# Placing attention, gates and slot copies on a fixed line of MoE half-steps, with the row-tiled work of a half in one step

## The chip, the cores and the metric

The kernel runs on one core of one Trainium2 chip. The metric is the device time of one execution in microseconds (us). A time quoted is the median of three to seven executions. The span that a profile page gives is about 1.7 us shorter than the device time of the same execution. Times inside an execution are counted from the start of its span.

Five engines share the work: PE (TensorE, matmuls), DVE (VectorE), ACT (ScalarE), POOL (GpSimd, which here also issues the loads of the experts' weights) and SP (SyncE, which issues the other transfers).

## The reference, cut to what matters

Eight sequences pass through an attention whose softmaxes are taken of q and of k apart. A gate then picks one expert for each sequence, and the sequence passes through the two matrices of that expert.

```python
def _attn_ref(q, k, v):                      # 8 sequences, 8 heads, 576 rows, 64 columns
    q_s = softmax of q over its 64 columns
    k_s = softmax of k over the 576 rows
    kv = np.einsum('bhsd,bhse->bhde', k_s, v)
    return np.einsum('bhsd,bhde->bhse', q_s, kv)

def _moe_ref(x, w_gate, w1, w2):             # x: 8 x 576 x 512, w1: 8 x 512 x 1024
    pooled = x.mean(axis=1)
    logits = pooled @ w_gate
    e_idx = np.argmax(logits, axis=1)        # one expert for each sequence
    ...
        h = np.maximum(x[mask] @ w1[e], 0.0)
        out[mask] = gate_w[mask, None, None] * (h @ w2[e])
```

The sequences pick the experts 2 3 3 1 3 3 4 6. So sequences 0, 1, 3, 6 and 7 need new weights. Sequences 2, 4 and 5 find theirs in the core's memory.

## The kernel before

A sequence is worked in two halves of four heads each. For a half, q, k and v are loaded; ACT takes exponentials, POOL casts v and scales q; PE forms k^T v (`kv_step`), transposes q (`t_step`) and multiplies both to x (`x_step`). DVE evacuates x and sums it for the gate. To evacuate is to copy a result out of the bank in which matmuls left it; the next matmul that needs this bank waits until then. The row sum, also on DVE, is the sum of q's exponentials over their 64 columns, by which POOL then scales q.

```python
    def t_step(n, g):                        # one partition half g of the half n
        eq = halves[n]["eq"]
        r = slice(64 * g, 64 * g + 64)
        tp = kv_banks(n)[g].bitcast(FP16)[:, 448:448 + S]
        for j in range(J):                   # J = 9
            nc.tensor.transpose(out=tp[:, 64 * j:64 * j + 64], in_=eq[r, j], identity=ident[r, r])
        ...
```

The gate finds the expert. If an earlier sequence has loaded the same expert, the loads are skipped by a condition. Five slots hold weights. Before the MoE block of sequence b, DVE copies the weights of its source slot into slot b % 5, in two parts for w1 and two for w2. The source slot is known only on the chip, so it is read by a register:

```python
    def gate_step(b):
        ...                                  # on DVE: the expert, and the slot that holds it
        nh = 1 if b else 2
        for fh in range(nh):
            for i in range(2):
                for h in range(2):
                    nc.gpsimd.dma_start(out=w1_all[..., slot, ...], in_=w1_src[i, h][...], **kw)
        ...                                  # then load_w2(b): two loads of w2; kw holds the condition

    def fetch(b, w_all, part):               # the slot copy
        ...
        cs = slice(part * half, (part + 1) * half)
        nc.vector.tensor_copy(
            out=w_all[:, b % NS, cs],
            in_=w_all[:, ds(seqs[b]["src"], 1), cs].rearrange("p o c f -> p (o c) f"),
        )
```

The MoE block is a generator of 17 half-steps. Between them, the program runs the attention, gate and copies that are due on a line of ticks, 12 ticks to a sequence. The order written here is the order of each engine's instructions.

```python
    NA = 12
    for b in range(B):
        for i in range(2 if b else 0):
            n, t0 = 2 * b + i, NA * b + 5 * i
            at(t0, kv_step, n)
            for g in range(2):
                at(t0 + 1 + g, t_step, n, g)
                at(t0 + 3 + g, x_step, n, g)
        at(NA * b + 10, gate_step, b)
        ...
            for part in range(2):
                at(NA * (b + 1) + 6 + part, fetch, b, w1_all, part)
                at(NA * (b + 1) + 8 + part, fetch, b, w2_all, part)
    for n in range(4, 2 * B):
        t0 = NA * (n // 2) + 5 * (n % 2)
        ...                                  # exp_q, cast_v, exp_k, load(n + 3), scale_q ahead of t0
    ...
        for b in range(B):
            for m, _ in enumerate(moe(b)):
                goal = NA * (b + 2) + 10     # attention two sequences ahead of MoE
                left = units - m
                tick = min(tick + max(0.7, (goal - tick) / left), NA * (b + 3))
                run_ticks(tick)
```

The copies of sequence b stand at ticks 12b + 18 to 12b + 21, and the gate of the next sequence at 12b + 22.

The softmax here doesn't subtract the row's maximum and nothing guards it: scores larger than these inputs give would overflow.

Of the kernel before, what the change touches and what calls it, by code (L numbers as in the profile page):

```python
# [19 lines left out]
def kernel(  # L20
# [54 lines left out]
    nc.vector.memset(ones_f32, 1.0)  # L75
    ones_row = consts.tile([1, 128], FP16)
# [3 lines left out]
    held = consts.tile([1, 8], FP16)  # L80
# [75 lines left out]
    def kv_step(n):  # L156
        ek, va, kps = halves[n]["ek"], v_aug[n % NVB], kv_banks(n)
        for j in range(J):
            for g in range(2):
                r = slice(64 * g, 64 * g + 64)  # L160
                nc.tensor.matmul(  # L161
                    kps[g][:, 0:129], lhsT=ek[r, j], rhs=va[r, j],
                    start=(j == 0), stop=(j == J - 1),
                )
        for g in range(2):
            icv = kv_pool.tile([128, 1], FP32, name="icv")
            nc.vector.reciprocal(out=icv, in_=kps[g][:, 0:1])
            kv = kv_pool.tile([128, 128], FP16, name="kv")
            nc.vector.scalar_tensor_tensor(
                out=kv, in0=kps[g][:, 1:129], scalar=icv, in1=blkmask, op0=ALU.mult, op1=ALU.mult,  # L170
            )
            halves[n]["kv"][g] = kv

    def t_step(n, g):
        eq = halves[n]["eq"]
        r = slice(64 * g, 64 * g + 64)
        tp = kv_banks(n)[g].bitcast(FP16)[:, 448:448 + S]
        for j in range(J):
            nc.tensor.transpose(out=tp[:, 64 * j:64 * j + 64], in_=eq[r, j], identity=ident[r, r])  # L179
        qt = qt_pool.tile([128, S], FP16, name="qt")  # L180
        if n < 2:
            nc.scalar.copy(qt, tp)
        else:
            nc.vector.tensor_copy(out=qt, in_=tp)  # L184
        halves[n]["qt"][g] = qt

    def x_step(n, g):
        b, i = divmod(n, 2)
        c = 2 * i + g
        if c == 0:  # L190
            xt = xt_pool.tile([128, ND, S], FP16, name="xt")
            pooled = gat_pool.tile([128, ND], FP32, name="pooled")
            seqs[b] = {"xt": xt, "pooled": pooled}
        xt, pooled = seqs[b]["xt"], seqs[b]["pooled"]
        kvs, qts = halves[n]["kv"], halves[n]["qt"]
        px = bank("x")
        nc.tensor.matmul(px[:, 0:SM], lhsT=kvs[g], rhs=qts[g][:, 0:SM], start=True, stop=True)  # L197
        nc.tensor.matmul(px[:, SM:S], lhsT=kvs[g], rhs=qts[g][:, SM:S], start=True, stop=True)  # L198
        nc.vector.tensor_tensor_reduce(  # L199
            out=xt[:, c, :], in0=px[:, 0:S], in1=ones_f32.to_broadcast([128, S]),  # L200
            scale=1.0, scalar=0.0, op0=ALU.mult, op1=ALU.add, accum_out=pooled[:, c:c + 1],
        )

    def gate_step(b):
        pooled = seqs[b]["pooled"]
        pg = bank("x")
# [61 lines left out]
    def hold_loads():  # L268

        nc.sync.dma_start(out=held, in_=w1_all[64:65, 0, ND - 1, 0:8])  # L270
# [97 lines left out]
    NA = 12  # L368
# [5 lines left out]
    for b in range(B):  # L374
        for i in range(2 if b else 0):
            n, t0 = 2 * b + i, NA * b + 5 * i
            at(t0, kv_step, n)
            for g in range(2):
                at(t0 + 1 + g, t_step, n, g)
                at(t0 + 3 + g, x_step, n, g)  # L380
        at(NA * b + 10, gate_step, b)
        late = 0 if b else 5
        at(NA * b + 11 + late, gate_exp, b)
        at(NA * b + 12 + late, gate_split, b)
        at(NA * b + 14 + late, gate_spread, b)
        if b:
            for part in range(2):
                at(NA * (b + 1) + 6 + part, fetch, b, w1_all, part)
                at(NA * (b + 1) + 8 + part, fetch, b, w2_all, part)
    at(15, load_w2, 0)  # L390
    for n in range(4, 2 * B):
        t0 = NA * (n // 2) + 5 * (n % 2)
        x = 3 if n == 4 else 0
        at(t0 - 6 + x, exp_q, n)
        at(t0 - 6 + x, cast_v, n)
        at(t0 - 5 + x, exp_k, n)
        if n + 3 < 2 * B:
            at(t0 - 5 + x, load, n + 3)
        at(t0 - 4 + (x and 2), scale_q, n, nc.gpsimd)
# [16 lines left out]
    with tc.manual_schedule(engines={ET.PE, ET.DVE, ET.Activation, ET.Pool, ET.SP}):  # L416

        exp_q(0)
# [6 lines left out]
        t_step(0, 0)  # L425
        t_step(0, 1)
# [4 lines left out]
        t_step(1, 0)  # L431
        t_step(1, 1)
        x_step(0, 1)
        kv_step(1)
        cast_v(2)
        x_step(1, 0)
        exp_q(2)
        x_step(1, 1)
        exp_k(2)
        run_ticks(11)  # L440
        hold_loads()
        load(4)
        scale_q(2, nc.vector)
        exp_q(3)
        run_ticks(13)
        exp_k(3)
        cast_v(3, True)
        load(5)
        run_ticks(15)
        scale_q(3, nc.vector)  # L450
        tick = NA + 6.0
        run_ticks(tick)
        load(6)
        for b in range(B):
            units = 17
            for m, _ in enumerate(moe(b)):
                goal = NA * (b + 2) + 10
                left = units - m
                tick = min(tick + max(0.7, (goal - tick) / left), NA * (b + 3))
                run_ticks(tick)  # L460
# [30 lines left out]
```

## Time and profile before

| | before |
|---|---|
| median, 3 runs | 232.39 us (231.48 to 233.29) |
| span of the profiled execution | 230.8 us |
| PE busy | 179.8 us, 78% of the span |
| start of MoE blocks 0, 1, 2, 3 | 32.5, 74.6, 95.8, 127.9 us |
| end of PE | 225.8 us |

The prediction shows the views that carry its argument. One more is needed for the comparison: the windows view of the kernel before, cut at the starts of single MoE blocks. Each line is a stretch and its length; then the busy time of PE, of PE's weight loads, of DVE, ACT and POOL, with instruction counts in brackets; then the granted PE clock (the share of TensorE's full clock that the profile shows as let through), the DMA share and GB/s.

```profile
74.55:95.77 21.22, 21.22 (x203) 11.17 (x202) 13.02 (x44) 12.62 (x20) 6.28 (x10) 0.99 0.75 222
127.85:149.70 21.85, 21.85 (x203) 11.32 (x203) 13.04 (x44) 12.62 (x20) 6.28 (x10) 0.96 0.51 147
149.70:171.20 21.50, 21.11 (x204) 11.14 (x203) 14.29 (x46) 12.62 (x20) 7.01 (x10) 1.00 0.41 116
171.20:193.50 22.30, 21.09 (x204) 11.12 (x203) 14.18 (x47) 10.62 (x18) 9.54 (x9) 1.00 0.79 151
193.50:209.92 16.42, 16.42 (x122) 8.33 (x123) 3.60 (x19) 8.79 (x16) 3.94 (x6) 1.00 0.82 140
```

Compare a line's length with PE's busy time. In these blocks (1 and 3 to 6) the two differ by at most 1.2 us, and the clock is nearly full. Here PE is the bound. Block 6, with no attention beside it, is 16.4 us, and the attention of a further sequence adds about 5 us.

### The profile page before, as it was taken

What the parts mean: (1) busy time and instruction counts of PE and PEld (TensorE: products, weight loads), DVE (VectorE), ACT (ScalarE), POOL (GpSimd) and SP (SyncE); (2) the same over time, 40 slices, a digit from 0 to 9 for tenths busy, and PEclk for the clock granted to TensorE, in tenths of its full rate; (3) what the DMA queues carried; (4) which work ended last, traced back from release to release, by engine and by line L of the source; (5) the groups of instructions that cost most, each with busy time, mean ns of one, the idle gap of its engine ahead of it and who ended that gap; (6) DMA issues with size and microseconds to landing.
All of it is one profiled execution on the core that took longest, in us unless ns stands there. A gap on an engine that the chain in (4) does not pass through costs nothing.

```text
span 230.8 us, 4509 instructions
## 1 busy us (share of the span) xinstructions
PE 179.8 (78%) x1608; PEld 94.4 (41%) x1608; DVE 113.9 (49%) x361; ACT 108.6 (47%) x167; POOL 68.7 (30%) x88
## 2 busy tenths in 40 slices
PE   0184369539934999999902999999999998999991
PEld 0152235314412554455401554555445544545540
DVE  0747965514617457765405565775676556120200
ACT  3686005450430755475510473666457423645631
POOL 1232910386202270369000443046126700600000
PEclk9999999855995999999985799999999999999998
DMA  6996799999999883989997164780254995599145
GB/s 207 382 394 250 101 156 289 396 342 275 294 296 363 261 301 84 288 232 256 276 287 272 23 199 151 200 273 4 58 128 74 169 231 119 97 181 268 31 94 112
DMA packets 28807, 48.55 MB, mean 210 GB/s; under 512 B 3184, under 2 KB 10352, under 8 KB 28784
## 3 DMA queue, kind: packets, MB, share of 16 engines
q1 hardware_dynamic: 19472, 37.76, 50.2%
q0 software_dynamic: 8736, 10.49, 27.9%
q8 instruction: 12, 0.20, 0.3%
q10 hardware_dynamic: 576, 0.02, 0.1%
q14 instruction: 11, 0.09, 0.1%
HBM read 61.88 MB, written 9.44 MB: 309 GB/s over the span
## 4 chain that ended last, share of the span: by engine, by line
PE 52%; DMA 28%; DVE 8%; issue 5%; SPq 1%; POOL 1%; POOLq 1%; ACT 1%; DVEq 0%
DMA w_all<-in_moe_w_dram 20%; PE mm L320 19%; PE mm L339 17%; DMA v_in<-in_v_dram 8%; DVE xt L199 3%; PE mm L354 3%; PE x L197 3%; PE kv L161 3%; PE kv L179 3%; PE ht L325 2%; DVE qs L143 2%; DVE w_all L306 1%; SPq L120 1%; PE x L208 1%; POOL w_all L255 1%
## 5 line engine op out<-in xcount | busy, mean ns | idle before, releaser
L320 PE MATMUL mm<-xt,w_all 128*128 128x512 f16 x256 | 67.5, 393 | 0.0
L339 PE MATMUL mm<-w_all,hsb 128*128 128x512 f16 x256 | 63.8, 388 | 0.0
L329 ACT ACTIVATE hsb<-mm 128x512 f16<-128x512 f32 x64 | 37.3, 590 | 37.6 <-PE mm L320 37.6
L146 POOL TENSOR_TENSOR eq<-eq,qsi 128x1152 f16<-128x1152 f16 x13 | 28.8, 2217 | 66.8 <-DVE qsi L145 60.4
L346 ACT ACTIVATE osb<-mm,gate 128x512 f32<-128x512 f32 x32 | 21.9, 686 | 44.2 <-PE mm L339 32.8
L306 DVE COPY w_all<-w_all 128x2048 f16 x28 | 19.1, 682 | 33.2 <-DMA w_all<-in_moe_w_dram 31.1
L199 DVE CUSTOM_DVE_ANT_0 xt<-x,ones_f 128x576 f16<-128x576 f32 x32 | 24.2, 755 | 18.0 <-PE x L198 18.0
L339 PEld LDWEIGHTS <-hsb 128*128 128x128 f16 x256 | 22.3, 99 | 25.2 <-issue 1.6
L197 PE MATMUL x<-qt,kv 128*128 128x512 f16 x32 | 14.0, 439 | 22.9 <-DVE pooled L199 21.4
L320 PEld LDWEIGHTS <-w_all 128*128 128x128 f16 x256 | 20.6, 100 | 20.1 <-issue 4.1
L179 PE MATMUL kv<-ident,eq 64*128 64x64 f16 x270 | 13.7, 200 | 16.7 <-DVE eq L146 9.3
L255 POOL DMA_DIRECT2D w_all<-in_moe_w_dram x36 | 15.1, 426 | 34.2 <-DVE hl L282 17.5
L133 POOL CAST va<-v_in 128x1152 f16<-128x1152 f32 x14 | 16.3, 1163 | 28.1 <-DMA v_in<-in_v_dram 27.9
L143 DVE TENSOR_REDUCE qs<-eq 128x18 f32<-128x1152 f16 x16 | 21.5, 1344 | 5.4 <-ACT eq L125 5.4
L325 PEld LDWEIGHTS <-w_all 128*128 128x128 f16 x256 | 16.6, 100 | 16.0 <-issue 1.6
L184 DVE COPY qt<-kv 128x576 f16<-128x576 f16 x28 | 12.7, 455 | 16.4 <-PE kv L179 16.4
L125 ACT ACTIVATE eq<-q_in 128x1152 f16<-128x1152 f32 x16 | 18.5, 1156 | 4.5 <-DMA q_in<-in_q_dram 4.5
L179 PEld LDWEIGHTS <-eq 64*128 64x128 f16 x288 | 11.1, 102 | 22.9 <-issue 14.8
L137 ACT ACTIVATE ek<-k_in 128x1152 f16<-128x1152 f32 x16 | 18.5, 1154 | 2.2 <-DMA k_in<-in_k_dram 2.2
L325 PE MATMUL ht<-xt,w_all 128*128 128x64 f16 x256 | 18.1, 194 | 0.0
L161 PE MATMUL kv<-va,ek 64*128 64x129 f16 x270 | 12.4, 243 | 4.2 <-POOL va L133 4.2
L359 ACT ACTIVATE osb_t<-mm,gate 128x256 f32<-128x256 f32 x8 | 3.8, 473 | 23.7 <-PE mm L354 23.7
(59 smaller groups left out, 120.8 us busy)
## 6 DMA issues: line engine op xcount, KB each, us to landing
q_in<-in_q_dram SPq DMA_DIRECT2D x16, 576.0 KB, 7.3
k_in<-in_k_dram SPq DMA_DIRECT2D x16, 576.0 KB, 8.9
v_in<-in_v_dram SPq DMA_DIRECT2D x16, 576.0 KB, 10.1
w_all<-in_moe_w_dram POOLq DMA_DIRECT2D x16, 512.0 KB
out_dram<-osb SPq DMA_DIRECT2D x64, 128.0 KB, 4.8
w_all<-in_moe_w_dram POOLq DMA_DIRECT2D x28, 256.0 KB
w_all<-in_moe_w_dram POOLq DMA_DIRECT2D x8, 128.0 KB
out_dram<-osb_t SPq DMA_DIRECT2D x16, 64.0 KB, 2.3
```

The source lines that it names most:

```text
L143: nc.vector.tensor_reduce(out=qs, in_=eq, op=ALU.add, axis=AX.X)
L146: eng.tensor_tensor(out=eq, in0=eq, in1=qsi.unsqueeze(3).to_broadcast([128, J, 2, Dh]), op=ALU.mult,)
L161: nc.tensor.matmul(kps[g][:, 0:129], lhsT=ek[r, j], rhs=va[r, j], start=(j == 0), stop=(j == J - 1),)
L179: nc.tensor.transpose(out=tp[:, 64 * j:64 * j + 64], in_=eq[r, j], identity=ident[r, r])
L197: nc.tensor.matmul(px[:, 0:SM], lhsT=kvs[g], rhs=qts[g][:, 0:SM], start=True, stop=True)
L199: nc.vector.tensor_tensor_reduce(out=xt[:, c, :], in0=px[:, 0:S], in1=ones_f32.to_broadcast([128, S]), scale=1.0, scalar=0.0, op0=ALU.mult ...
L306: nc.vector.tensor_copy(out=w_all[:, b % NS, cs], in_=w_all[:, ds(seqs[b]["src"], 1), cs].rearrange("p o c f -> p (o c) f"),)
L320: nc.tensor.matmul(phm, lhsT=w1_sb[:, c, fsl], rhs=xt[:, c, 0:SM], start=(c == 0), stop=(c == ND - 1),)
L325: nc.tensor.matmul(pht[:, fc * ST:(fc + 1) * ST], lhsT=w1_sb[:, c, fsl], rhs=xt[:, c, SM:S], start=(fc == 0 and c == 0), stop=(fc == NF - ...
L329: nc.scalar.activation(out=hsb[:, fc, 0:SM], in_=phm, func=AF.Relu)
L339: nc.tensor.matmul(po, lhsT=hsb[:, fc, st * 128:st * 128 + 128], rhs=w2_sb[:, fc, :], start=(fc == 0), stop=(fc == NF - 1),)
L346: nc.scalar.mul(osb, po, gate)
```

## The change

Its intent is to bring every piece of work to a chosen place on a line of MoE half-steps, 17 to a block, instead of letting the attention run two sequences ahead. Four other things change with it. The transposes of both partition halves become one alternating group behind k^T v. Gate 0 works from sums of q, so that it needs no x. The loads of sequence 2 and of the first half of sequence 3 are held to the end of MoE 0. A warm-up of 55 matmuls stands at the start. Smaller moves in the first two sequences (some evacuations go from DVE to ACT, the order ahead of MoE 0 is another) are not in the cut. The diff, cut to its core:

```diff
-    def t_step(n, g):
+    def t_mm(n):
+        eq, kps = halves[n]["eq"], kv_banks(n)
+        for j in range(J):
+            for g in range(2):
+                r = slice(64 * g, 64 * g + 64)
+                tp = kps[g].bitcast(FP16)[:, 448:448 + S]
+                nc.tensor.transpose(out=tp[:, 64 * j:64 * j + 64], in_=eq[r, j], identity=ident[r, r])
...
+    def kvt_step(n):
+        kv_mm(n)
+        t_mm(n)
+        for g in range(2):
+            kv_out(n, g)
+            t_out(n, g)
...
+    def q_sum_step(n):                       # sums of q for gate 0, by one-column matmuls
...
+    NU = 17
+    def at_gate(t, b):
+        at(t, gate_step, b)
+        at(t + 1, gate_exp, b)
+        at(t + 2, gate_split, b)
+        at(t + 4, gate_spread, b)
+
+    at_gate(2, 1)
+    for b in range(2, B):
+        u = 24 if b == 2 else 34 + 15 * (b - 3)
+        for i in range(2):
+            n, t = 2 * b + i, u + 4 * i
+            at(t, kvt_step, n)
             for g in range(2):
+                at(t + 2 + g, x_step, n, g)
+            at(t - 4.2, exp_q, n)
+            at(t - 4.2, cast_v, n)
+            at(t - 3.2, exp_k, n)
+            if n + 3 < 2 * B:
+                at(t - 3.2, load, n + 3)
+            at(t - 2.8, scale_q, n, nc.gpsimd)
+        at_gate(u + 8, b)
+    for b in range(1, B):
+        for part in range(2):
+            at(NU * b - 2 + part, fetch, b, w1_all, part)
+            at(NU * b + 0.5 + part, fetch, b, w2_all, part)
...
         for b in range(B):
-            units = 17
             for m, _ in enumerate(moe(b)):
-                goal = NA * (b + 2) + 10
-                left = units - m
-                tick = min(tick + max(0.7, (goal - tick) / left), NA * (b + 3))
-                run_ticks(tick)
+                run_ticks(NU * b + m + 1)
+            if b == 0:
+                for n in (4, 5, 6):
+                    load(n)
```

On the new line the w1 copies of sequence b stand at 17b - 2 and 17b - 1, its w2 copies at 17b + 0.5 and 17b + 1.5. The gates 2 to 7 stand at 32, 42, 57, 72, 87 and 102.

## The prediction

> **What bounds the kernel now.** I read the page's busy table first, then the windows view cut at the starts of the experts' MoE blocks, then the waits, the chain, and the timelines of PE, DVE, POOL and SP. The windows view (stretch, its length, then busy us of PE, PEld, DVE, ACT, POOL, then granted clock, DMA share, GB/s):
>
> ```profile
> 0.00:32.47 32.47, 11.70 (x146) 7.65 (x147) 19.94 (x57) 15.35 (x17) 11.95 (x22) 1.00 0.86 252
> 32.47:74.55 42.08, 28.37 (x227) 14.26 (x225) 19.18 (x60) 14.41 (x21) 12.30 (x12) 0.76 1.09 317
> 74.55:127.85 53.30, 43.44 (x405) 22.80 (x404) 28.24 (x91) 25.23 (x40) 17.66 (x21) 0.92 0.87 246
> 127.85:225.80 97.95, 96.32 (x837) 49.74 (x836) 46.50 (x156) 53.14 (x88) 26.78 (x35) 0.99 0.60 137
> 225.80:230.80 5.00, 0.00 (x0) 0.00 (x0) 0.00 (x0) 0.47 (x1) 0.00 (x0) 0.78 0.44 97
> ```
>
> The last 98 us before the drain are bound by PE (98% busy). The first 128 us are not: PE works 83.5 of 127.85 us, while the DMA engines are busy 0.86 to 1.09 of the time. So two different limits lie in a row, and only the first is worth tens of us. The waits view says who blocks:
>
> ```profile
> DVE w_all L306 <- DMA w_all<-in_moe_w_dram: 31.1, 6, 9.4
> POOL va L133 <- DMA v_in<-in_v_dram: 27.9, 4, 14.4
> PE x L197 <- DVE pooled L199: 21.4, 5, 9.5
> ```
>
> Read together: DVE stands in a slot copy (L306) until an expert's weights land, the evacuation of x (L199) stands behind it, and PE stands behind that. PE's timeline shows the worst two cases:
>
> ```profile
> 72.14 0.58 PE L197 MATMUL x<-qt,kv 128*128 128x512 f16 x1 [6.73 <-DVE pooled L199]
> ...
> 125.36 0.59 PE L197 MATMUL x<-qt,kv 128*128 128x512 f16 x1 [9.46 <-DVE pooled L199]
> ```
>
> And POOL's timeline shows why the second expert's weights came late: POOL waited for a v load before it reached the issue at L255.
>
> ```profile
> 43.91 1.17 POOL L133 CAST va<-v_in 128x1152 f16<-128x1152 f32 x1 [14.39 <-DMA v_in<-in_v_dram]
> 45.43 1.33 POOL L255 DMA_DIRECT2D w_all<-in_moe_w_dram  x2 [0.36 <-issue]
> ```
>
> From the reference, the eight sequences pick experts 2 3 3 1 3 3 4 6; so sequences 0, 1, 3, 6, 7 load weights (5 loads; the POOL queue's 10.49 MB is 5 of 2.1 MB) and 2, 4, 5 reuse a slot.
>
> **What the Trainium skill says.** (1) "TensorEngine Tiling (Array Packing)", Key Properties: different tiles can load and multiply in parallel, and a change of tiling mode drains TensorE. The trace agrees: four L320 matmuls take 0.86 us on the chain in a plain stretch and 0.97 before a row-tiled group, so a drain of about 0.11. The k^T v group, which already alternates the halves, runs 18 matmuls of 129 columns in 0.64 us (35 ns each), below the 54 ns that 129 columns need at the page's 2.4 GHz. The transposes, one half at a time, take 0.37 us for 9 (41 ns each). (2) "TensorE: Matmul & The Clock Gate", Part 1: the array starts at half clock and needs about 3.4 us of sustained work. The trace agrees: the same group of 18 takes 1.16 us early and 0.70 late, and L320 x4 takes 1.89 after the 9.46 us stall against 1.04. (3) "DMA: Bandwidth & Descriptors", Issuing engines are not separate DMA queues: all DMAs share 16 engines and interleave. The trace agrees: sequence 3's weights, under two sets of q/k/v loads, land 23.6 us after their first issue (100.3 to 123.94); sequence 7's, beside outputs only, 16 us (197.4 to 213.4). (4) "PSUM — Partial Sum Buffer", Engine vs sequencer instructions: ScalarE, VectorE and GpSimd queues are strict FIFO, which is the blocking seen above.
>
> **The change part by part.** I follow the new program order of each engine with the durations above. A MoE block alone is 15.85 us (L354 to L354, 208.93 to 224.78 on the chain): 8 units of 0.98, 8 half-steps of 0.87, one of 0.99.
>
> *Merged row-tiled groups.* Before, a half pays 0.64 + 2x0.37 and three drains of 0.11 = 1.71 us. After: 0.64, 18 alternating transposes at 30 ns (estimate, between the 35 ns measured for k^T v and the 25 ns floor that the Clock Gate page gives) = 0.54, one drain = 1.29. That saves 0.4 us a half, 12 halves inside MoE: **5 us** of PE. Against it: DVE starts the half's four evacuations (2 x (0.16+0.35+0.46) = 2.0 us) only when the group ends, and in the first half of each sequence the next half's row sum (1.35+0.27) is placed ahead of x's evacuation. DVE: 2.0 + 1.6 + 0.8 = 4.4 us from the group's end to the free x bank; PE: two or three units plus x = 3.1. A new stall of about 1.2 us, five times in the stretches below: **6 us**. These cancel.
>
> *q-sum gate first, warm-up.* Sequence 0's gate now needs only k^T v of both halves and the sums of q (36 one-column matmuls, 8 tiny DVE ops), not the four x evacuations. V lands as before (ACT casts the second half's at 13.23 to 14.4), so k^T v ends near 16.5, its DVE work 17.6, the pooled sum 18.5, the expert index 19.7; before 21.76. First weight issue 21.1 for 23.09; the first half of w1 took 7.15 us to land (23.09 to the hold's release at 30.24), so 28.2. By then the four halves of sequences 0 and 1 are through (DVE's two scalings of 3.0 us each, one after the other from 20, end at 27). MoE 0 starts at **28.3** against 32.47. The 55 warm-up matmuls end before the first transposes at 9.35 and are off the path; they buy some warm clock.
>
> *Loads held to the end of MoE 0; gate 1 at its unit 2.* No q/k/v runs from 23 to 47, so w of sequence 0 (16 us) lands by 38, in time. MoE 0: 28.3 + 15.85 + 2 x's 0.5 + gates 0.9 + cold start 1.2 = 46.8. Gate 1 follows unit 2 at 32.5; with 1.7 us of DVE and 1.4 to issue, w of sequence 1 is issued at 35.6 instead of 45.4: w1 near 46 to 47, w2 near 53 (before: 70.7). Copies 1.4: MoE 1 starts at **48.4**, before 74.55. But attention of sequence 2 is not yet done, and its loads are issued only at 47.8. By the analogous burst before (issued from 31.1: k landing at 41.63, v at 43.9, next q at 45.8) q lands at 55, k 58, v 58.5. ACT stands in the exponential of q between two evacuations, PE runs out of its three banks: 4.3 us; the transposes wait for POOL's scaling (61.8): 1.1; the second half 1.3. MoE 1 ends at 48.4 + 15.85 + 4.3 + 1.1 + 1.3 + attention 4.3 = 75.2.
>
> *Gate 2 at the last half-step.* Its DVE chain (2 us), the register read (about 1) and the two w1 copies (1.4) follow each other before MoE 2 can start, with 1 us of PE work beside them: start at **78**, before 96.
>
> *Gate 3 at half-step 42, its copy at 49.* Gate 3 falls at 78 + 7.84 + 0.87 + attention of sequence 3, 4.3 = 91; issue at 93.5. With the same two sets of loads and outputs in flight as before, w1 lands 12.2 us later (100.3 to 112.55 before): 105.7, copies to **107**. MoE 2 is over at 100. So PE stands 7 us, turns cold (1.5), and waits about 2.5 more for w2 inside MoE 3 (23.6 us after issue: 117). MoE 3 ends at 107 + 15.85 + 4.8 + 1.5 + 2.5 = 131.7. Before, it started at 127.85.
>
> *The rest.* Gates 4 and 5 load nothing; gates 6 and 7 are 13 and 15 half-steps ahead of their copies, 13 us and more against the 8.5 (197.4 to 205.9) that w1 of sequence 7 took: hidden. PE-bound: 4 x 15.85 = 63.4, attention 2.5 x 4.3 = 10.8, DVE stalls 3 x 1.2 = 3.6. PE ends at 209.5, plus the 5.0 of drain as before = 214.5 span, plus 1.6 (232.4 to 230.8 before) = 216. I take **214**, since I may have counted twice where stalls overlap.
>
> **Rivals.** (a) The weights of sequence 3 cost nothing: if loads do not collide with them, they land 8.5 us after issue, MoE 3 starts at 103 and w2 does not block; and the DVE stalls are hidden. Then 203 to 206. For it: the case of sequence 7. Against: the loads at half-steps 45.8 and 49.8 fall right there. (b) The attention feed becomes the bound: loads start after MoE 0, so each of ACT, POOL and DVE waits for it in order. All DMA work is 50.2% + 27.9% of 230.8 us = 180 us of the 16 engines; in 214 us that is 84%, and one badly placed load costs 5 to 10 us: 222 to 228. For it: the waits of POOL on v, up to 14.4 us before. (c) The gain of the early part is given back wholly, because before was two sequences ahead in attention when it reached its PE-bound end: the 98 us would become longer by the attention left over. I have counted 0.5 sequence for that; a whole one more costs 4.3 us.
>
> **Range and chances.** Rival (a) sets the lower end at 204, half of (b) the upper at 224. Within 2% needs over 227.7, 14 us more than I find.
>
> **What would show it.** First L320 near 28; MoE 1 starting near 48, MoE 3 near 107; x18 transposes at about 0.55 us; DVE's slot-copy wait falling for sequence 1 and staying near 10 us for sequence 3; ACT waiting for q loads near 52; PE waits on x's bank of about 1 us each. Wrong if the loads after MoE 0 land far later, or if weights overlap loads without loss.

## The result and the profile after

The changed kernel takes **256.41 us** (median of 4 runs, 256.19 to 258.73), the kernel before 232.84 us in the same rounds (4 runs, 231.48 to 233.77). The ratio is 1.104 (95% interval 1.0953 to 1.1127): slower. A ratio is the mean time of one kernel's fast runs over that of the other's of the same rounds, so not quite the ratio of the medians.

The table sets the starts of the MoE blocks side by side. The last three columns are experiments that are told below.

| us from the span's start | predicted | before | after | e1 | e5 | e8 |
|---|---|---|---|---|---|---|
| MoE 0 | 28.3 | 32.5 | 29.4 | 29.5 | 29.8 | 29.5 |
| MoE 1 | 48.4 | 74.6 | 47.2 | 47.3 | 48.1 | 47.3 |
| MoE 2 | 78 | 95.8 | 80.3 | 80.3 | 82.0 | 81.2 |
| MoE 3 | 107 | 127.8 | 111.1 | 112.7 | 113.6 | 112.5 |
| MoE 4 | 131.7 | 149.7 | 145.1 | 146.0 | 146.3 | 138.2 |
| MoE 7 | | 209.9 | 233.3 | 215.9 | 209.4 | 201.3 |
| end of PE | 209.5 | 225.8 | 249.2 | 231.8 | 225.3 | 217.3 |

The early part came as predicted within about 4 us: MoE 1 starts 27 us earlier than before, MoE 3 17 us earlier. At MoE 4 only 4.6 us of that are left, at MoE 6 it is 5 us behind, and at MoE 7 23 us behind. The windows view of the kernel after, cut at the block starts (columns as above), shows where:

```profile
47.15:80.33 33.18, 21.55 (x202) 10.89 (x200) 15.93 (x42) 16.39 (x24) 10.02 (x11) 0.92 1.06 363
80.33:111.06 30.73, 23.17 (x238) 12.52 (x239) 16.53 (x57) 13.87 (x21) 12.26 (x12) 0.92 0.68 182
111.06:145.05 33.99, 24.43 (x206) 11.97 (x206) 17.67 (x50) 12.62 (x20) 8.84 (x11) 0.85 0.73 222
145.05:172.33 27.28, 22.58 (x237) 12.05 (x237) 16.33 (x54) 12.68 (x20) 6.77 (x10) 0.94 0.50 164
172.33:198.79 26.46, 22.35 (x206) 11.22 (x206) 14.86 (x48) 12.53 (x20) 10.41 (x10) 0.94 0.60 115
198.79:233.34 34.55, 19.07 (x122) 9.02 (x122) 7.47 (x26) 8.36 (x16) 3.95 (x6) 0.75 0.51 92
233.34:249.20 15.86, 15.86 (x114) 7.90 (x112) 0.00 (x0) 8.50 (x14) 0.00 (x0) 1.00 0.33 76
```

Blocks 3 to 5 take 34.0, 27.3 and 26.5 us, where before they took 21.9, 21.5 and 22.3. PE is idle for 4 to 10 us in each, and the clock is below full in each. Block 6 takes 34.6 us against 16.4 before, with the same 122 matmul records, a clock of 0.75 and 15.5 us of idle PE. Only block 7, which has nothing beside it, runs as before (15.86 us).

The waits view of PE after (engine, line, what it waited for: us in total, times, longest) answers to the waits shown of before:

```profile
PE x L352 <- DVE hl L344: 14.7, 1, 14.7
PE mm L381 <- DVE w_all L367: 13.1, 6, 6.1
PE x L221 <- DVE qt L191: 5.5, 1, 5.5
PE kv L183 <- POOL eq L147: 5.2, 5, 1.4
PE x L221 <- DVE pooled L232: 4.5, 5, 1.1
PE kv L162 <- POOL va L134: 4.4, 3, 1.9
PE mm L381 <- ACT hsb L390: 4.2, 1, 4.2
```

The long waits of before for x's evacuation (21.4 us in five) have become 4.5 us. In their place stand one wait of 14.7 us, six at or just after block starts for the slot copy (L367), single ones of 5.5 and 4.2 us, and many of 1 to 2 us. Read alone, the first line says that PE waits for a tiny DVE operation of the gate. DVE's timeline says what that operation stood behind (start, duration, instruction, in brackets the idle time ahead of it):

```profile
202.63 0.13 DVE L296 TENSOR_SCALAR nmx<-mx 1x1 f32<-1x1 f32 x1
217.94 1.42 DVE L367 COPY w_all<-w_all 128x2048 f16 x2 [15.18 <-issue]
...
219.64 0.20 DVE L344 TENSOR_SCALAR hl<-hl,gt 1x1 f16<-1x1 f16 x1
```

DVE finishes gate 7's index at 202.76 us, then stands for 15.18 us before a slot copy. That copy brings the w2 of sequence 6 into place. Those weights were there already: in e1, below, the same copy runs at 199.13 us without a wait. The releaser is printed as "issue", which means that the view found none. The source view of the copies and POOL's timeline give it:

```profile
L367 DVEq EVENT_SEMAPHORE  x24: 21/21/15295, 43.7 to 220.9; - x24
```

```profile
203.72 2.76 POOL L314 DMA_DIRECT2D w_all<-in_moe_w_dram  x4 [9.03 <-DVE nmx L296]
206.59 0.77 POOL L325 DMA_DIRECT2D w_all<-in_moe_w_dram  x1
207.63 0.75 POOL L325 DMA_DIRECT2D w_all<-in_moe_w_dram  x1 [0.27 <-issue]
```

One of the 24 semaphore waits of L367 in DVE's queue lasted 15,295 ns (the numbers are least, median and greatest), where the median is 21 ns. It ends when the weights of sequence 7 have landed, which POOL issued from 203.72 us on. So the copy for sequence 6 waits for the weights of sequence 7. PE's timeline gives the price:

```profile
219.89 0.16 PE L352 MATMUL x<-hl,ones_row 1*128 1x2 f16 x1 [14.74 <-DVE hl L344]
219.98 1.89 PE L381 MATMUL mm<-xt,w_all 128*128 128x512 f16 x4
```

After the wait, four matmuls take 1.89 us instead of 1.04: PE resumes at half clock.

Why should the copy wait for the next sequence's weights? Its source is read by a register and may be any of the five slots. The packed trace agrees: this copy of the kernel after waits on four DMA semaphores, its counterpart in the kernel before (190.66 us) and in e1 on two. On the line of half-steps these two w2 copies (102.5 and 103.5) are the only ones that stand behind the next sequence's gate (102), and the loads follow the gate. That the register is the reason is read from the program; a copy with a fixed source was not run.

### The profile page after: what moved, and what is told of

It reads as the page before. It is cut to its first block, busy times and chain, and to the rows that moved or that the text cites. A ratio compares the mean times of both kernels' runs of the same rounds, so it can differ in the third digit from the quotient of the medians.

```text
span 254.6 us, 4684 instructions
## 1 busy us (share of the span) xinstructions
PE 184.9 (73%) x1703; PEld 98.3 (39%) x1703; DVE 112.3 (44%) x357; ACT 113.7 (45%) x177; POOL 68.1 (27%) x88
## 3 DMA queue, kind: packets, MB, share of 16 engines
q0 software_dynamic: 8736, 10.49, 25.6%
## 5 line engine op out<-in xcount | busy, mean ns | idle before, releaser
L381 PE MATMUL mm<-xt,w_all 128*128 128x512 f16 x256 | 75.6, 426 | 17.7 <-DVE w_all L367 13.1
L400 PE MATMUL mm<-w_all,hsb 128*128 128x512 f16 x256 | 59.4, 379 | 0.0
L381 PEld LDWEIGHTS <-w_all 128*128 128x128 f16 x256 | 22.2, 106 | 58.2 <-issue 28.5
L367 DVE COPY w_all<-w_all 128x2048 f16 x28 | 20.8, 748 | 41.3 <-DMA w_all<-in_moe_w_dram 25.1
L314 POOL DMA_DIRECT2D w_all<-in_moe_w_dram x36 | 15.2, 427 | 76.2 <-DMA w_all<-in_moe_w_dram 34.1
L147 POOL TENSOR_TENSOR eq<-eq,qsi 128x1152 f16<-128x1152 f16 x13 | 27.8, 2139 | 27.1 <-DVE qsi L146 21.9
L386 PEld LDWEIGHTS <-w_all 128*128 128x128 f16 x256 | 17.7, 105 | 18.2 <-issue 5.6
L232 DVE CUSTOM_DVE_ANT_0 xt<-x,ones_f 128x576 f16<-128x576 f32 x26 | 19.4, 744 | 12.2 <-PE x L222 12.2
L144 DVE TENSOR_REDUCE qs<-eq 128x18 f32<-128x1152 f16 x16 | 21.5, 1345 | 6.4 <-ACT eq L126 6.4
L386 PE MATMUL ht<-xt,w_all 128*128 128x64 f16 x256 | 19.2, 201 | 0.0
L170 DVE RECIPROCAL icv<-kv 128x1 f32<-128x1 f32 x30 | 4.9, 162 | 30.3 <-PE kv L183 29.0
L162 PEld LDWEIGHTS <-ek 64*128 64x128 f16 x288 | 11.3, 110 | 11.3 <-issue 9.1
L183 PE MATMUL kv<-ident,eq 64*128 64x64 f16 x270 | 7.8, 203 | 8.5 <-POOL eq L147 5.2
L352 PE MATMUL x<-hl,ones_row 1*128 1x2 f16 x8 | 1.4, 171 | 14.7 <-DVE hl L344 14.7
```

What stands on the lines that cost most here:

```text
L144: nc.vector.tensor_reduce(out=qs, in_=eq, op=ALU.add, axis=AX.X)
L147: eng.tensor_tensor(out=eq, in0=eq, in1=qsi.unsqueeze(3).to_broadcast([128, J, 2, Dh]), op=ALU.mult,)
L162: nc.tensor.matmul(kps[g][:, 0:129], lhsT=ek[r, j], rhs=va[r, j], start=(j == 0), stop=(j == J - 1),)
L232: nc.vector.tensor_tensor_reduce(out=xt[:, c, :], in0=px[:, 0:S], in1=ones_f32.to_broadcast([128, S]), scale=1.0, scalar=0.0, op0=ALU.mult ...
L367: nc.vector.tensor_copy(out=w_all[:, b % NS, cs], in_=w_all[:, ds(seqs[b]["src"], 1), cs].rearrange("p o c f -> p (o c) f"),)
L381: nc.tensor.matmul(phm, lhsT=w1_sb[:, c, fsl], rhs=xt[:, c, 0:SM], start=(c == 0), stop=(c == ND - 1),)
```

## The experiments

The theories, with the letters that the expectations use:

- **A**: the w2 copies of sequence 6, behind gate 7 in program order, wait for sequence 7's weights. This costs 15 us and more.
- **B**: the attention's feed (exponentials, cast, scaling) is placed too tightly ahead of its use, and PE waits for POOL and DVE.
- **C**: it is the order on DVE at block starts that costs: slot copies and a row sum stand ahead of the evacuations which PE needs.
- **F**: q, k and v loads placed beside sequence 3's weights draw those weights out.
- **G**: gate 3 comes too late.

The remaining letters in the texts concern the merged group and the half clock after a gap; each text says what it means by them.

Each result is the median of four runs, with the ratio to the kernel before in the same rounds and its 95% interval. In these ratios the profiled run is left out. A run over 1.5% above the fastest of its kernel counts as slow: one run of e7, one of e8, two of e4, and one of the kernel before in the rounds of e8 to e11. The medians have these runs in. By fast runs alone the median is 224.78 us for e8 and 230.31 for e7. The ratio of e4 rests on its two slow runs, since the fastest run was the profiled one; its two fast runs alone give 1.096. The runs were made in four batches on different chips; the kernel before had medians of 233.2, 232.5, 232.4 and 232.1 us in them, so differences of some tenths of a us between batches mean nothing.

| run | built from | median us | ratio to before |
|---|---|---|---|
| after | | 256.41 | 1.104 [1.095, 1.113] |
| e1_copy6_early | after | 239.21 | 1.029 [1.021, 1.037] |
| e2_feed_early | after | 252.75 | 1.085 [1.077, 1.093] |
| e3_halves_apart | after | 256.39 | 1.100 [1.092, 1.108] |
| e4_no_warm | after | 257.11 | 1.108 [1.100, 1.116] |
| e12_both | e1 and e2 | 238.12 | 1.023 [1.015, 1.030] |
| e6_keep_busy | e1 | 235.29 | 1.011 [1.004, 1.017] |
| e5_order | e1 | 231.73 | 0.998 [0.990, 1.007] |
| e8_loads_held | e5 | 225.47 | 0.971 [0.962, 0.980] |
| e9_gate3_early | e8 | 224.67 | 0.969 [0.961, 0.977] |
| e13_held_busy | e8 | 224.73 | 0.970 [0.964, 0.977] |
| e7_merge_in_before | before | 230.81 | 0.993 [0.985, 1.001] |
| e10_copy6_late_in_before | before | 248.35 | 1.067 [1.058, 1.075] |
| e11_loads_held_in_before | before | 224.19 | 0.964 [0.957, 0.971] |
| e14_before_held_merged | e11 and e7 | 221.77 | 0.955 [0.947, 0.963] |

All of them computed the right result.

### e1_copy6_early: the copy of sequence 6 ahead of gate 7

```diff
-            at(NU * b + 0.5 + part, fetch, b, w2_all, part)
+            at(NU * b - 0.8 + part * 0.4 if b == 6 else NU * b + 0.5 + part, fetch, b, w2_all, part)
```

> The changed kernel, with one edit: the w2 slot copy of sequence 6 is placed ahead of gate 7 instead of behind it. Theory A: the copy reads its source slot by a register, so it waits for every load of w2 placed ahead of it in the program; behind gate 7 these include sequence 7's own load (issued 203.7 to 208.4, landed near 217.9). Then the 15.2 us of DVE ahead of that copy and the 14.7 us of PE ahead of the spread of gate 7 vanish, with about 2 us of half clock after it: 256.4 becomes 238 to 242. Rival: sequence 6's own load was late (issued 180.8 to 185.2, landing after 200); then DVE stands at the moved copy instead and the time stays above 250.

Measured: 239.21 us, 17.2 us less than the changed kernel. DVE's timeline of this run has three copies in one piece and without a wait, the last of w1 and both of w2:

```profile
199.13 2.02 DVE L367 COPY w_all<-w_all 128x2048 f16 x3
```

PE's timeline of the same run shows the matmul that had waited 14.74 us, now without a wait and followed at full clock:

```profile
204.83 0.17 PE L352 MATMUL x<-hl,ones_row 1*128 1x2 f16 x1
204.93 1.04 PE L381 MATMUL mm<-xt,w_all 128*128 128x512 f16 x4
```

Theory A is shown: one placement cost 17.2 us, the wait itself and the half clock behind it.

### e10_copy6_late_in_before: the same fault made in the kernel before

```diff
-                at(NA * (b + 1) + 8 + part, fetch, b, w2_all, part)
+                at(NA * (b + 1) + 8 + part + (2.5 if b == 6 else 0), fetch, b, w2_all, part)
```

> The kernel before with only the w2 copy of sequence 6 moved behind gate 7, the fault of the changed kernel put into the other one. Theory A says that it is the placement alone that costs: DVE then waits for sequence 7's weights (16 us from first issue), PE for the spread of gate 7 behind DVE; 8 to 14 us slower than before. Rival: only the changed kernel's crowding made it hurt; within 2 us.

Measured: 248.35 us, 16 us more than the kernel before, so somewhat above what had been expected. DVE's timeline:

```profile
212.27 1.42 DVE L306 COPY w_all<-w_all 128x2048 f16 x2 [15.29 <-issue]
```

The kernel before, with everything else as it was, gets the same wait (15.29 against 15.18 us) by the same placement. This removes the doubt that something else of the change takes part in it.

### e2_feed_early: the attention's feed earlier

```diff
-            at(t - 4.2, exp_q, n)
-            at(t - 4.2, cast_v, n)
-            at(t - 3.2, exp_k, n)
+            e = 0 if b < 4 else (2 if i else 4.0)
+            at(t - 4.2 - e, exp_q, n)
+            at(t - 4.2 - e, cast_v, n)
+            at(t - 4.0 - e if e else t - 3.2, exp_k, n)
             if n + 3 < 2 * B:
-                at(t - 3.2, load, n + 3)
-            at(t - 2.8, scale_q, n, nc.gpsimd)
+                at(t - 4.0 - e if e else t - 3.2, load, n + 3)
+            at(t - 3.2 - e if e else t - 2.8, scale_q, n, nc.gpsimd)
```

> The changed kernel, with one edit: for sequences 2 to 7 the exponentials, the cast of v and the scaling of q of a half are placed 2 (second half) or 4 (first half) half-steps earlier for n of 4 and up, so that POOL has them before the gate of the sequence ahead and DVE's row sum no longer stands between the evacuations of the first half and x. Theory B: the line leaves POOL and DVE too little slack, which costs PE 1 to 3 us at each first half (waits on va, eq and the x bank: 5.2 + 4.4 + 4.5 us in the trace) and half clock after them; the time falls by 8 to 15 us. Rival: these waits are covered by the wait for weights that follows, and the time stays within 3 us.

Measured: 252.75 us. The gain of 3.7 us is less than half of what B expected. The waits for POOL went, but others took their place: PE's waits for the gate's operations on DVE rose from 14.7 us in one to 20.6 us in five, and gate 3's loads came later, since POOL now had a scaling ahead of them.

### e12_both: e1 and e2 together

The edit is that of e1 and that of e2.

> Both edits of the first two runs together. If theories A and B hold and are independent: 256.4 less 16 less 8 to 15, so 225 to 233, about even with the kernel before (232.8). If B's waits are covered, 238 to 242 as with the first edit alone.

Measured: 238.12 us, 1.1 us less than e1 alone. Beside e1 the earlier feed is worth next to nothing. Gate 3's loads are issued at 104.13 us here against 101.29 in e1, and PE's longest wait for a slot copy, ahead of MoE 3, is 7.5 us where e1 has 1.3 there. So what the feed gains behind them is lost ahead of them. Theory B largely falls: the trouble is no simple lack of time ahead, but an order in which each piece moved forward stands in another's way.

### e3_halves_apart: the merge undone

```diff
-        for j in range(J):
-            for g in range(2):
+        for g in range(2):
+            for j in range(J):
                 r = slice(64 * g, 64 * g + 64)
```

> The changed kernel with only the merge of the transposes undone: all nine of one half, then all nine of the other, in the same place. In the trace the merged 18 took about 0.36 us on the path against 2 x 0.37 apart, so 16 halves lose 0.35 each: 3 to 6 us slower if PE's own time counts; within 1 us if the waits set the time and swallow it.

Measured: 256.39 us, no change. In PE's timeline of the kernel after, a merged half is this:

```profile
67.73 0.70 PE L162 MATMUL kv<-va,ek 64*128 64x129 f16 x18
68.27 0.43 PE L183 MATMUL kv<-ident,eq 64*128 64x64 f16 x18
68.63 1.04 PE L400 MATMUL mm<-w_all,hsb 128*128 128x512 f16 x4
```

From their start to the next work the 18 alternating transposes take 0.36 us; in e3 the same 18, one half after the other, take 0.52 us (69.10 to 69.62). PE saves 0.16 us a half, some 2 us for the 12 halves inside MoE. The medians don't show it, and the runs of e3 spread over 3.2 us: a part of the 2 us could hide in that. The merge did what it was to do on PE, and the 3 to 6 us that were expected if PE's own time counts are not there.

### e7_merge_in_before: the merge alone, in the kernel before

```diff
+    def t_pair(n):
+        ...                                  # the 18 transposes with j outside, g inside; then both evacuations
...
+            if b > 1:
+                at(t0 + 1, t_pair, n)
             for g in range(2):
-                at(t0 + 1 + g, t_step, n, g)
+                if b == 1:
+                    at(t0 + 1 + g, t_step, n, g)
```

> The kernel before with only the merge added: transposes of both halves of 12 halves as one group one tick after k^T v, nothing else moved. Before is bound by PE in its last 98 us, with 6 to 8 such halves in them. Each saves one drain of 0.11 and about 0.36 of transposes: 2.5 to 4 us faster than before in all. Rival: the pair needs the DVE for both evacuations at once and x waits, so within 1 us.

Measured: 230.81 us, ratio 0.993 [0.985, 1.001]. The gain of about 1.7 us (2.2 without the slow run) is less than the interval settles, so this run alone decides nothing; e14 below repeats the comparison.

### e4_no_warm: without the warm-up

```diff
-        warm(55)
```

> The changed kernel without its 55 warm-up matmuls. They end near 7.3 us, 2 us before the first transposes, and the early k^T v groups still take 1.16 us each (half clock) with them. Theory: they buy under 0.5 us, and 256.4 stays within 1 us. Rival: without them the early groups and the first MoE block run longer at half clock and the time rises by 2 to 4 us.

Measured: 257.11 us against 256.41, with runs from 253.4 to 258.67; the two fast ones took 253.4 and 256.29. No effect can be told from that spread. The warm-up isn't the cause of the loss, and no gain of it is shown.

### e6_keep_busy: dummy matmuls in the gaps at block starts

```diff
         for b in range(B):
+            warm({2: 90, 3: 20, 4: 20, 5: 20}.get(b, 0))
```

(Built on e1.)

> The first edit and dummy matmuls of 128 columns in the known gaps of PE: 90 ahead of MoE 2 (gap 6.1 us), 20 each ahead of MoE 3, 4 and 5 (gaps 1.3 to 2.5 us). They add no dependency of the real work on anything new. Theory D: after each gap PE runs at half clock for 2 to 4 us, though most gaps are under 2 us; keeping PE busy in them saves 4 to 7 us: 232 to 235. Rival: the half clock comes of something else, or its loss is hidden behind the next wait; then 238 to 241.

Measured: 235.29 us, 3.9 us less than e1. PE's timeline of e1 at the start of block 2, where the gap is left empty:

```profile
80.27 1.89 PE L381 MATMUL mm<-xt,w_all 128*128 128x512 f16 x4 [6.08 <-DVE w_all L367]
...
82.30 1.16 PE L162 MATMUL kv<-va,ek 64*128 64x129 f16 x18
```

And of e6, where dummy matmuls fill most of it:

```profile
74.17 5.20 PE L333 MATMUL ht<-blkmask,ident 128*128 128x128 f16 x90
80.33 1.33 PE L383 MATMUL mm<-xt,w_all 128*128 128x512 f16 x4 [0.96 <-DVE w_all L369]
...
81.71 0.70 PE L162 MATMUL kv<-va,ek 64*128 64x129 f16 x18
```

The block starts at the same moment, but the first four matmuls take 1.33 us instead of 1.89 and the group of 18 takes 0.70 instead of 1.16. So the waits at block starts are paid twice: once as a wait, once as half clock after it, and the second part is 3.9 us here by the medians (2.7 between the two profiled runs).

### e5_order: slot copies and one row sum earlier

Built on e1. For sequences from 4 on, the slot copies come 3 half-steps earlier. For sequences from 3 on, the feed of the second half comes 2 earlier, so that its row sum no longer stands between the evacuations of the first half.

```diff
-            at(t - 4.2, exp_q, n)
+            e = 2 if i and b > 2 else 0
+            at(t - 4.2 - e, exp_q, n)
...                                           # cast_v, exp_k, load and scale_q likewise
-            at(NU * b - 2 + part, fetch, b, w1_all, part)
-            at(NU * b + 0.5 + part, fetch, b, w2_all, part)
+            at(NU * b - (5 if b > 3 else 2) + part, fetch, b, w1_all, part)
+            at(NU * b - 2.5 + part if b > 3 else NU * b + 0.5 + part, fetch, b, w2_all, part)
```

> The first edit (w2 copy of sequence 6 ahead of gate 7, 239.2 us) and two more: the second half's exponentials, cast and row sum come 2 half-steps earlier, so that the row sum is not between the first half's evacuations and x; and the slot copies of sequences 4 to 7 come 3 half-steps earlier, off the start of the MoE block. Theory C: the rest of the loss in MoE 3 to 5 is DVE order at the block's start (waits of 1.0 to 1.8 us at x's bank and at the copies, 7 us in all, and half clock after them, some 5 us); then 228 to 234. Rival: the waits only move, as they did when the feed alone was moved (252.8 and 238.1 us); then 237 to 240.

Measured: 231.73 us, 7.5 us less than e1. PE's waits at block starts for the slot copy fall from six (12.3 us in e1) to two (8.7 us), and from MoE 4 to the end of PE 79.0 us are left of e1's 85.8. The time is what theory C forecast. The parts of the edit (slot copies, row sum and, with the feed, some loads) were not run apart, so which of them brings how much is not shown.

One case of a slow copy is to be seen in the changed kernel itself. DVE's timeline:

```profile
142.69 2.30 DVE L367 COPY w_all<-w_all 128x2048 f16 x1
...
145.59 0.68 DVE L367 COPY w_all<-w_all 128x2048 f16 x1
```

POOL's timeline in the same moment:

```profile
142.32 2.12 POOL L147 TENSOR_TENSOR eq<-eq,qsi 128x1152 f16<-128x1152 f16 x1 [2.96 <-DVE qsi L146]
```

The first copy takes 2.30 us instead of 0.68, and ends 0.55 us after POOL's scaling does. The Trainium skill, "SBUF — State Buffer", Who interferes with whom, says that a DVE copy in a two-port mode and GpSimd exclude each other for a whole instruction and that the loser blocks fully. The trace agrees: the copy loses 1.6 us to a scaling of 2.12 us that began 0.37 us before it. The mode of this copy is not in the trace.

### e8_loads_held: the q, k and v loads after sequence 3's weights

Built on e5. The loads of two halves are held until after the last slot copy of sequence 3.

```diff
-                at(t - 4.0 - e if e else t - 3.2, load, n + 3)
+                at(52.7 + n - 8 if n in (8, 9) else t - 4.0 - e if e else t - 3.2, load, n + 3)
```

> The kernel of e5_order (231.7 us) with one more edit: the two sets of q/k/v loads that were issued beside the weights of sequence 3 (104.3 to 111 there) are held until after its last slot copy. Theory F: they are what stretched these weights (w1 landed 10.4 us, w2 22.7 us after the first issue); alone they land in about 8.5 and 16 us, so PE's wait of 5.7 us for DVE inside MoE 3 shrinks to under 1 and the time falls by 4 to 7 us. Rival: the output DMAs and the weights' own rate set the landing, and the time stays within 1.5 us of e5_order.

Measured: 225.47 us, 6.3 us less than e5 and 3% less than the kernel before. DVE's timeline of e5, where the weights of sequence 3 are issued at 102.08 us:

```profile
124.83 0.69 DVE L367 COPY w_all<-w_all 128x2048 f16 x1 [7.88 <-DMA w_all<-in_moe_w_dram]
```

And of e8, with the issue at 101.05 us:

```profile
118.08 0.69 DVE L367 COPY w_all<-w_all 128x2048 f16 x1 [2.15 <-DMA w_all<-in_moe_w_dram]
```

The line is the first w2 copy, in brackets its wait for the weights. From the first issue to the landing of w2 it is 22.7 us in e5 and 17.0 us in e8. The wait of PE for x in MoE 3 (5.7 us in e5) is gone, and block 3 takes 25.6 us instead of 32.7. Theory F is shown.

### e11_loads_held_in_before: the same in the kernel before

```diff
-            at(t0 - 5 + x, load, n + 3)
+            at({9: 57.5, 10: 58.5}.get(n, t0 - 5 + x), load, n + 3)
```

> The kernel before with the two sets of loads issued at 100.9 and 113.2, beside the weights of sequence 3, held until after its slot copies. By theory F the weights land in 16 us instead of 23.6, and PE's 9.46 us wait at 125 shrinks to about 2: 6 to 8 us faster than before. Rival: within 2 us, or slower because the held loads are then late for the next attention.

Measured: 224.19 us, ratio 0.964. PE's timeline shows what became of the wait of 9.46 us before block 3 that the prediction quotes:

```profile
116.25 0.38 PE L197 MATMUL x<-qt,kv 128*128 128x512 f16 x1 [0.72 <-DVE pooled L199]
```

The weights land 15 us after their issue (99.92 to 114.83) instead of 23.6. So the gain is no property of the new line: two displaced loads alone are worth 8.2 us in the kernel before.

### e9_gate3_early: gate 3 three half-steps earlier

Built on e8: the two halves of sequence 3 are put at half-steps 33 and 35 with their feed in the last half-steps of MoE 1, gate 3 at 39, and the later sequences at 46, 63, 77 and 93.

```diff
-        u = 24 if b == 2 else 34 + 15 * (b - 3)
+        u = (0, 0, 24, 33, 46, 63, 77, 93)[b]
...
-            n, t = 2 * b + i, u + 4 * i
+            n, t = 2 * b + i, u + (2 if b == 3 else 4) * i
...
-        at_gate(u + 8, b)
+        at_gate(u + (6 if b == 3 else 8), b)
```

> e8_loads_held with attention of sequence 3 moved up: its first half just ahead of MoE 2 (where PE stands 6 to 7 us), its second half two half-steps later, gate 3 at 39 instead of 42; the later sequences one or two half-steps closer to it. Theory G: the distance of 9 half-steps from gate 3 to MoE 3 was too short for a load of 16 to 23 us; this should take away most of what PE still waits at MoE 2 and 3: 4 to 9 us below e8_loads_held, 217 to 224 us, clearly faster than before. Rival: DVE and POOL at the block's start get more crowded, the waits move, and the time stays within 2 us of e8_loads_held.

Measured: 224.67 us against 225.47 (224.78 by the fast runs of e8): no difference, as the rival had it. Gate 3's loads were issued at 100.21 us instead of 101.05, because PE waited for what had been moved forward: 1.9 us ahead of MoE 2 for the scaling on POOL, and 3.4 us inside it for the gate on DVE. So for this placing the waits moved. The attempt didn't bring the loads much earlier, so it says nothing for or against theory G. This stays open.

### e13_held_busy: dummy matmuls on e8

```diff
         for b in range(B):
+            warm({2: 100, 3: 22}.get(b, 0))
```

> e8_loads_held (225.5 us) with dummy matmuls in its two largest remaining gaps: 100 ahead of MoE 2 (gap 7.0 us), 22 ahead of MoE 3 (1.5 us). By theory D the blocks then start at full clock: 2 to 4 us faster, 221 to 223.5. Rival: what follows waits for DVE anyway; within 1 us of e8_loads_held.

Measured: 224.73 us, the same as e8 by its fast runs (224.78), where 2 to 4 us less had been expected. The half clock did go where the dummies stand: the 256 matmuls of w1 take 67.7 us instead of 70.0, and MoE 2 and MoE 3 are 0.7 and 0.8 us shorter. But MoE 4 is 1.3 us longer. Ahead of it both runs have the same gap of 2.02 us in front of an x matmul; after it four matmuls take 1.89 us here (from 136.69 us on) and 1.03 in e8 (from 138.16 on). So half clock came back at a gap that had been left open, and why it did so here and not in e8 is not known.

### e14_before_held_merged: both good parts in the kernel before

The edit is that of e11 and that of e7.

> The kernel before with the loads held (224.2 us alone) and the transposes of both halves merged (230.8 us alone). With the weight stall gone nearly all of the last 130 us are bound by PE, and 10 halves at about 0.35 to 0.45 us count: 220 to 222. If the evacuation of the pair delays x as much as it saves: 223.5 to 225.

Measured: 221.77 us, ratio 0.955 [0.947, 0.963]: 2.4 us less than e11, and the fastest version. It beats the kernel before by 4.5% and the changed kernel by some 35 us. The merge adds about 2 us to e11, as e7 had indicated; the intervals of e11 and e14 still overlap a little, so the size of that part isn't settled.

## Why the prediction was wrong, point by point

The prediction gave 209.5 us for the end of PE, and 249.2 were measured. By its own stages the 39.7 us divide thus: 4.1 until the start of MoE 3, 9.3 in MoE 3 (34.0 instead of 24.7), and 26.4 from MoE 4 to the end (104.2 instead of 77.8).

**The step that failed most is "The rest"**, and in it the sentence that gates 6 and 7 are "13 and 15 half-steps ahead of their copies ... hidden". The distances from each gate to its own copy were right. What wasn't asked is what else a copy waits for. The copies of sequence 6 stand behind gate 7, and wait for sequence 7's weights. e1 takes 18.4 us out of this stage (104.2 to 85.8) and 17.2 out of the whole, and e10 makes the same loss in the other kernel. None of the three rivals contained it.

**The term "DVE stalls 3 x 1.2" was too small.** It counted x's bank, with the row sum ahead of the evacuation, and those waits came as said (five, 4.5 us, the longest 1.1). It left out the slot copies at block starts, POOL's scaling (three waits of 1.0 to 1.4 us in MoE 4 and 5) and the half clock after such waits. e5 takes out 6.8 us of this stage by placing the slot copies and the row sum earlier. With e1 and e5 the stage from MoE 4 on is 79.0 us against the predicted 77.8: the sum comes near once these causes are away.

**MoE 3's term was right in kind and wrong in size.** The prediction had 1.5 us of half clock and 2.5 us of waiting for w2. The wait was 5.5 us, and shorter waits that it hadn't counted came to 4.0 (1.1 for POOL's scaling, 1.0 for x's bank, 1.8 for the next slot copy at the end). PE's busy time was 24.4 us where the prediction's terms give 22.2 with the half clock in, since half clock came twice. The loads collide as said: w1 landed 10.5 us after its issue (predicted 12.2), w2 22.4 us after (predicted 23.6). Rival (a), that they do not collide, falls. With the loads held (e8), block 3 takes 25.6 us. Here the prediction had taken the collision as given, where the experiments show it to be a matter of placing.

**The start of MoE 3 is nearer than its parts.** Gate 3's loads were issued at 99.77 us, 6.3 later than the predicted 93.5; the landing 1.7 us sooner made a part of that good. So it is in part luck that 111.1 lies only 4.1 from 107.

**The start of MoE 2 was 2.3 us late**, since the gap ahead of it was 6.1 us instead of the 2.8 that the prediction has (75.2 to 78). Two parts can be read. DVE's timeline of the kernel after, in gate 2:

```profile
74.91 1.79 DVE L281 TENSOR_TENSOR same<-hist,eidx 1x8 f32<-1x8 f32 x1
...
79.58 1.42 DVE L367 COPY w_all<-w_all 128x2048 f16 x2 [2.07 <-DMA w_all<-in_moe_w_dram]
```

The first line is an operation on 8 numbers that takes 0.15 us in gate 7 and 1.79 us here; POOL's scaling runs from 74.57 to 76.69, and it ends with it. The second shows the copy waiting 2.07 us for loads that this sequence skips: POOL passes the four conditional loads of w1 one after the other, 0.46 us apart, from 78.08 to 79.45. Neither part was tried on the chip by itself.

**What came as predicted:** MoE 0 and MoE 1 within 1.3 us; the first weight issue at 21.05 us (predicted 21.1); ACT's wait for q, which costs PE 4.2 us in MoE 1 (predicted 4.3); the x bank; the collision of loads. The merged group was better than thought: 0.90 us from its start to the next work (0.54 for k^T v, 0.36 for the transposes), where 0.64 + 0.54 and a drain of 0.11 had been worked out. Two readings behind that sum were wrong. On the chain, the L320 matmuls of 0.97 us stand behind row-tiled or other short groups and not before one. And the floor of 25 ns doesn't hold for matmuls that alternate between the halves (last section). A switch does cost something: in the kernel before, it is 0.21 us from the start of four L325 to a row-tiled group (80.70 to 80.91) and 0.11 to plain matmuls (79.72 to 79.83).

**Why it is slower than before although MoE 1 starts 27 us earlier.** Rival (c) named the direction, that the early gain is given back since the kernel before is two sequences ahead in attention, but valued it at 4.3 us. The kernel before waits early and then has 98 us of work in which PE is idle for 1.6 us in all. The changed kernel ties each block to copies, gates and feed placed close to it. Blocks 3 to 5 take 88 us against 66 before, and block 6 adds 18.

**What is left.** e8 ends PE at 217.3 us, 7.8 after the predicted 209.5: 5.5 of it at the start of MoE 3, 0.9 in MoE 3 and 1.3 after. The first is the gap at gate 2 and a late gate 3, which e9 failed to test. The rest of the difference between 225.47 and 214 is the 2 us that the prediction took off its own sum of 216, and the spread of the runs (the profiled run of e8 took 223.78).

## What to carry to other kernels

The slot copies, whose source a register chooses, wait for loads into slots that they do not read (15.2 and 15.3 us); so place such a copy ahead of the next load into that memory, and for each placing ask not only whether its own data are there but what else stands ahead of it in the program. A line of fixed places is only as good as its closest pair: list for every engine what follows what, and look there for short operations that PE needs behind long ones that may wait. When a transfer sets a start, hold other transfers back before moving work around: two displaced loads gave 3 to 4% here, more than the whole reordering.

## What the Trainium skill lacked or had wrong

- "TensorE: Matmul & The Clock Gate" gives, under Wait — 56ns, not 53.3ns?, a floor of about 25 ns from start to start for small matmuls, however small, and names no exception there. Transposes that alternate between the partition halves go below it: in the packed trace of the kernel after, the starts of one merged group (68.27 us) lie 3 to 4 ns and 25 to 26 ns apart in turn; the nine of one half in the kernel before (80.91 us) lie 28 to 30 ns apart but for the first. Part 3 of the same page has the small step, about 4 ns for matmuls on different tiles, so it is the one sentence that lacks the exception.
- The same page's table ties the fall to half clock to an idle window of about 3.4 us; its section on a second failure mode has short idles that do it in another kernel, without a length. In the kernel after, half clock (four matmuls in 1.90 us, from 174.00 us on) followed a gap of only 1.71 us. A gap of 2.02 us was followed by full clock in e8 (four in 1.03 us) and by half clock in e13 (1.89 us). So a gap shorter than the window can cost clock, and need not.
- No page has it that a copy with a source chosen by a register can wait for loads of the same tensor that it doesn't read: 15.2 us here, 15.3 us in e10. That the register is the reason is not shown.
- "SBUF — State Buffer" has the exclusion of DVE and GpSimd, and the runs agree (a slot copy of 2.30 instead of 0.68 us, an operation on 8 numbers of 1.79 instead of 0.15 us beside POOL's scaling). It has no figure for what this costs a kernel in which POOL scales beside gates and copies.
- "DMA: Bandwidth & Descriptors" says that all transfers share the engines, without a figure for a mixed case: weights of one expert took 22.4 to 23.6 us beside two sets of q, k and v loads, and 15 to 17 us when these were held.
- No page has the time that POOL spends on a load skipped by its condition: about 0.46 us from one to the next, 2.3 us from the first to the sixth in gate 2 (78.08 to 80.35 us).
